# Reading a resident filter in place: a strided moving operand instead of packed copies in an FFT convolution beside a feed-forward block

## The chip, the cores and the metric

The kernel runs on one core of one Trainium2 chip. The metric is the device time of one execution in microseconds; the time of a kernel is the median over several runs.

## The reference

Two branches start from the same input and are added to it. Branch A gates a shifted input with `v`, convolves it along the sequence with a filter as long as the sequence, and gates the result with the normalised input. Branch B is a feed-forward block with ReLU. S = 2048 positions, D = 576 channels, Dff = 4608, all in float32.

```python
x = A_q
xn = layernorm(x)                       # no scale, no shift
# branch A
k_shift = sum(shift(k, t) * shift_k[:, 3 - t])  # causal, 4 taps
kv = k_shift * v
y = irfft(rfft(kv, 2*S) * rfft(ssm_k, 2*S))[:S] + kv * ssm_D
a = xn * y
# branch B
b = relu(xn @ w1) @ w2                  # 576 -> 4608 -> 576
out = x + a + b
```

## The kernel before, in words

Branch B fills TensorE (PE) from the start to the end. It runs in 36 "quads" `g` (18 slices of Dff, for each half of the positions). Each quad computes hidden values into the PSUM tiles `psh` (from the operands `x`, `xs`, `hl` and the split weights `wa` to `wd`, `wr`), splits them with ACT into `hh` and with DVE into `ll`, and multiplies them with the split second weight `w` into `pso`; DVE or ACT adds that to `acc`. Weights come on POOL's DMA queue (`load_w1`, `load_w2`) and are split by ACT (L512) and POOL (L513). DVE adds the weight sums (L525) and, at L684, `u`, which ACT at L686 and L591 needs before PE can go on with the next `psh`. L669 copies `psh` into `p`. L722 and L742 move `acc` into PSUM and back for some units.

Branch A is a generator, `conv()` with `stages()`. It runs between the matmuls of branch B: `tick` counts the columns that PE is given (`clock["ffn"]`) and takes the next step of the generator when its share is due. A step that yields a positive number costs so much of the share; a negative number is a pause of so many columns (`PAUSE` is 16,000); the word "wide" asks for a place where a PSUM slot can be borrowed. `here()` ties a step's instructions behind the latest ones of branch B on DVE and ACT.

All working memory of branch A is one SBUF tile, `area`, cut by offset into views that change from stage to stage. The stages that matter here:

- **Filter transform.** The filter lies resident in `kt`, as 288 channels by `A2` = 32 time residues, the residue innermost: element `t2` of all channels is a column with a step of 32 floats, 128 bytes. The two halves of the partitions hold the two halves of the channels. The loop over the 32 elements copies one after the other (odd ones on DVE at L918, even ones on ACT at L920) into one of four packed buffers `copies[e]`. Eleven filter groups follow behind the copies, each of up to 864 columns of the 32 x 288: `group` transforms them with float32 matmuls of 64x64 (L762) and the matrices `mats` into two PSUM tiles `psf` and the borrowed pair `psg`. ACT (L844) and DVE (L846) copy the results into the one buffer `z`, and SP's queue stores `z` to `zk` in HBM (L887). A piece of a group that ends at an element's border is split: 288 and 144 columns make up a full half of 432.
- **Input transform.** `load(t)` brings rows of `k` and `v` on ACT's queue for t up to 1 and on SP's after that, and for t up to 0 a row of `shift_k` on POOL's. These rows lie over `kt`. `tap` (L938, L941, L942) and `gate` (L946) make the gated input on DVE, and `input_group` transforms it through the same `group`, with stores to `zx` (L954).
- The products, the way back and the output follow; the change does not touch them.

`load(0)` stands behind the last copy of the filter, ahead of the last two filter groups in the code; the other loads come after the last group.

Of the kernel before, what the change touches and what calls it, by code (L numbers as in the profile page):

```python
# [12 lines left out]
AF = mybir.ActivationFunctionType  # L13
# [8 lines left out]
KS = 4  # L22
T = S // P
NH = D // 2
# [14 lines left out]
A2 = U * T  # L39
# [15 lines left out]
CW = 512  # L55
NCH = NG * D // CW
KG = 432
# [8 lines left out]
KT = 0  # L66
ROWS = 2 * KS + 8
REST = ROWS * D
Z, KSO, WT = REST, REST + 4 * CW, REST + 4 * CW + 4 * NH
AREA = WT + 4 * U * P  # L70

OPERANDS = ("00", "01", "s2", "s3", "11", "s1", "s4")
# [27 lines left out]
def h3_ffn_kernel(ctx: ExitStack, tc, x, k, v, shift_k, ssm_k, ssm_D, w1, w2, fwd, inv, mid, out):  # L100
    nc = tc.nc
    x = x[0].rearrange("(p u t) d -> u p t d", u=U, t=T)
    k = k[0].rearrange("(p u t) d -> u p t d", u=U, t=T)
# [28 lines left out]
    def at_t(z, t):  # L132

        return z[:, t].rearrange("q g d -> g q d")
# [5 lines left out]
    def fft_psum():  # L140
        return ps_f.tile([P, 512], F32, tag="f", name="psf")
# [4 lines left out]
    def borrowed():  # L146

        return ps_o.tile([P, 2, 512], F32, tag=f"o{slot['closed']}", name="psg")
# [12 lines left out]
    def move(tile_, rows, t, store=False, queues=(nc.sync, nc.sync)):  # L161
        for u in range(U):
            a, b = tile_[halves(u)[0]], rows[u, :, t]
            queues[u].dma_start(*((b, a) if store else (a, b)))
# [87 lines left out]
    @contextmanager  # L252
    def here():


        with tc.issue_after(done["acc"].ins), tc.issue_after(done["act"].ins):
            yield
# [502 lines left out]
    def in_turn(ps, a, m, start, stop):  # L760
        with tc.issue_after(done["pe"].ins):
            done["pe"] = nc.tensor.matmul(ps, a, m, start=start, stop=stop, skip_group_check=True)  # L762
# [35 lines left out]
    def stages(view, views):  # L798


        kt = view(KT, NH, A2)
# [6 lines left out]
                with here():  # L808
                    nc.scalar.dma_start(kt[halves(h)[0], d:d + KD, :], src)  # L809

        z = view(Z, 2, 2 * CW)
        mats = Ring(*views(WT, 4, U, P))

        def load_mat(key, t):
            nc.gpsimd.dma_start(mats.put(key), fwd[t])

        def group(parts, most, engines):


            wide = borrowed()  # L820
            sets = [[fft_psum() for _ in range(2)], [wide[:, r, :] for r in range(2)]]
            ends = []
            for pieces, banks in zip(parts, sets):
                off = 0
                for w, mat, src in pieces:
                    for k in range(2):
                        for r in range(2):
                            in_turn(banks[r][sides[r ^ k], off:off + w],
                                    mat(r)[sides[r], A1 * (r ^ k):A1 * (r ^ k) + A1],
                                    src[sides[r]], off == 0, True)  # L830
                    off += w
                ends.append(off)
            if ends[-1] < NH or len(ends) == 1:
                unwritten.add(slot["closed"])
            for n, off in enumerate(ends):
                to = z[:, :, n * most:n * most + off]
                if n and engines == ("act", "act"):
                    with here():
                        nc.scalar.activation(to, wide[:, :, :off], AF.Copy)
                    continue  # L840
                for r in range(2):
                    with here():
                        if engines[r] == "act":
                            nc.scalar.activation(to[:, r, :], sets[n][r][:, :off], AF.Copy)  # L844
                        else:
                            nc.vector.tensor_copy(to[:, r, :], sets[n][r][:, :off])  # L846

        def divided(a, b, most, step):

            parts = []  # L850
            while a < b:
                end, off = min(a + most, b), 0
                parts.append([])
                while a < end:
                    e, c = divmod(a, step)
                    w = min(end - a, step - c)
                    parts[-1].append((e, c, w, off))
                    a, off = a + w, off + w
            return parts
# [4 lines left out]
            yield -KT_GAP  # L864
        for t in range(2):
            load_mat(("k", t), t)
        copies = Ring(*views(KSO, 4, NH))
        skip = copies.put("skip")
        for h in range(2):
            nc.sync.dma_start(skip[h * A1:h * A1 + 1, :], ssm_D[None, h * NH:(h + 1) * NH])  # L870
        yield -PAUSE
# [4 lines left out]
        order = [T * u + t for t in range(T) for u in range(U)]  # L876
        flat = A2 * NH
        starts = list(range(0, flat, 2 * KG))

        def filter_group(a):  # L880
            parts = divided(a, min(a + 2 * KG, flat), KG, NH)
            group([[(w, lambda r, u=order[e] // T, t=order[e] % T: mats["k", t][:, u, :],
                     copies[e][:, c:c + w]) for e, c, w, _ in part] for part in parts],
                  KG, ("act", "dve"))
            for e, c, w, off in divided(a, min(a + 2 * KG, flat), flat, NH)[0]:
                for r in range(2):
                    nc.sync.dma_start(at_t(zk, order[e])[:, :, r * NH + c:r * NH + c + w],  # L887
                                      z[:, r, off:off + w])
# [4 lines left out]
        sums = Ring(*rows[11:15])  # L893
        terms = Ring(*rows[15:16])

        def load(t):

            w = win[t] if t < 2 else win.put(t)
            if t <= 0:
                nc.gpsimd.dma_start(sk[:, -t, :], shift_k[-t:1 - t, :].to_broadcast([P, D]))  # L900
            if t >= 0:
                queues = (nc.sync if t > 1 else nc.scalar,) * 2
                with here():
                    move(w, k, t, queues=queues)
                    move(gates.put(t), v, t, queues=queues)
            else:
                with here():
                    nc.vector.memset(w[0:1, :], 0.0)
                    nc.scalar.dma_start(w[1:A1, :], k[1, 0:A1 - 1, T + t, :])
                    nc.scalar.dma_start(w[A1:, :], k[0, :, T + t, :])  # L910
# [1 line left out]
        for t in range(1 - KS, 2):  # L912
            win.put(t)
        for e, t2 in enumerate(order):
            to = copies.put(e)
            with here():
                if e % 2:
                    nc.vector.tensor_copy(to, kt[:, :, t2])  # L918
                else:
                    nc.scalar.activation(to, kt[:, :, t2], AF.Copy)  # L920
            if e == A2 - 1:
                load(0)
            yield W_FK / 2
            while starts and min(starts[0] + 2 * KG, flat) <= e * NH + (e == A2 - 1) * NH:
                yield "wide"
                filter_group(starts.pop(0))
                yield W_FK / 2 / (len(range(0, flat, 2 * KG)) / A2)
            if e % U and e // U + 2 < T:
                load_mat(("k", e // U + 2), e // U + 2)
# [14 lines left out]
        def gate(t):  # L944
            with here():
                nc.vector.tensor_tensor(sums[t], sums[t], gates[t], OP.mult)  # L946

        def input_group(j):
            parts = divided(2 * j * CW, 2 * (j + 1) * CW, CW, D)
            group([[(w, lambda r, t=t: mats["x", t][:, r, :], sums[t][:, c:c + w])  # L950
                    for t, c, w, _ in part] for part in parts], CW, ("act", "act"))
            for t, c, w, off in divided(2 * j * CW, 2 * (j + 1) * CW, T * D, D)[0]:
                for r in range(2):
                    nc.sync.dma_start(at_t(zx, T * r + t)[:, :, c:c + w], z[:, r, off:off + w])  # L954

        for t in (*range(-1, -KS, -1), 1):
            load(t)
            yield -PAUSE / 4
        for t in range(2):
# [3 lines left out]
        for t in range(T):  # L963
            for n in range(KS + 1):
                if n < KS:
                    tap(t, n)
                    yield W_FX * (2 if n else 1)
                else:
                    gate(t)
                    if t + 2 < T:  # L970
                        load(t + 2)
                    yield W_FX
                if n == 1 or t == T - 1 and n == KS:
                    last = t if n == KS else t - 1
                    while made_groups < n_groups and (2 * CW * (made_groups + 1) - 1) // D <= last:
                        yield "wide"
                        input_group(made_groups)
                        made_groups += 1
                        yield 2 * W_FX
                    if n == 1 and 2 <= t + 1 < T:  # L980
                        load_mat(("x", t + 1), t + 1)
# [108 lines left out]
        order = [*range(HT, T), *range(HT)]  # L1090
# [213 lines left out]
```

## Time and profile before

| | |
|---|---|
| median of 3 runs | 1029.08 us (1028.98 to 1030.45) |
| profiled execution, own time | 1038.15 us |
| its span, first to last instruction | 1036.3 us |
| mean granted TensorE clock | 0.996 |
| PE busy | 1019.9 us, 98% of the span |
| DVE, ACT, POOL busy | 702.4, 431.4, 463.6 us |
| L920, 16 copies on ACT | 11.7 us, mean 731 ns |
| L918, 16 copies on DVE | 9.3 us, mean 591 ns |

A row of a group reads: line, engine, operation, output tile, input tiles, shape, count, then busy time in us and the mean of one in ns, then the idle time of the engine ahead of it and what ended it. Rows of a timeline begin with the start and the duration in us. PEld is the loading of weights, which overlaps PE. A row of the chain has start, duration and what ran. Matmuls of 64x64 on different corners of the array run side by side, so their durations overlap.

### The profile page before, as it was taken

To read this page: it belongs to the slowest core of one execution; us is meant where nothing else is said; L and a number is where in the kernel's file an instruction comes from. 1 tells how busy PE (TensorE), PEld (TensorE's weight loads), DVE (VectorE), ACT (ScalarE), POOL (GpSimd) and SP (SyncE) were. 2 spreads that over 40 slices of the span, in tenths; PEclk is the share of its full clock that TensorE was granted. 3 is DMA by queue.
4 is the path that set the end of the run, shared out by engine and by line. 5 is a ranking of instruction groups with operands and counts; after the bars stand their busy time and mean duration, and the time that the engine had idled before them with its cause. 6 is when DMAs were issued, how large, how long until landed. Compare 5 with 4: busy or idle time off the path is not lost.

```text
span 1036.3 us, 17434 instructions
## 1 busy us (share of the span) xinstructions
PE 1019.9 (98%) x6506; PEld 846.6 (82%) x6506; DVE 702.4 (68%) x1075; ACT 431.4 (42%) x770; POOL 463.6 (45%) x502
## 2 busy tenths in 40 slices
PE   8999999999999999989999999999999999999997
PEld 5898999998988888878878888866777777788777
DVE  6787677775565556778787889455666666556764
ACT  7244334443354444434444444544444445332120
POOL 3335444555443555544555455314424245244450
PEclk9999999999999999998999999999999999999999
DMA  7114364479445473379944433677877887757684
GB/s 175 52 49 118 114 162 126 154 216 199 115 127 172 160 245 104 126 216 322 277 139 132 129 103 115 210 221 227 242 212 226 250 256 226 221 177 230 208 259 114
DMA packets 130848, 184.69 MB, mean 178 GB/s; under 512 B 69213, under 2 KB 81631, under 8 KB 129868
## 3 DMA queue, kind: packets, MB, share of 16 engines
q1 hardware_dynamic: 76180, 123.48, 39.9%
q0 software_dynamic: 16048, 52.44, 16.9%
q10 hardware_dynamic: 38536, 7.66, 3.9%
q8 instruction: 51, 0.84, 0.3%
q14 instruction: 33, 0.27, 0.1%
HBM read 119.04 MB, written 45.61 MB: 159 GB/s over the span
## 4 chain that ended last, share of the span: by engine, by line
PE 88%; DMA 4%; DVE 3%; ACT 2%; issue 1%; POOL 1%; ACTq 1%; SPq 0%; DVEq 0%; POOLq 0%
PE pso L569 40%; PE psh L569 34%; PE psf L762 6%; PE psg L762 4%; PE psh_c L569 3%; DMA r<-in_w 2%; DMA zk<-area 1%; DMA acc<-in_x 1%; ACTq L809 0%; DVE area L1047 0%; DVE area L941 0%; DVE area L942 0%; ACT x L291 0%; DMA area<-in_k 0%; DVE sums L525 0%
## 5 line engine op out<-in xcount | busy, mean ns | idle before, releaser
L569 PE MATMUL pso<-w,hh 128*128 128x288 f32 x2304 | 467.9, 296 | 0.0
L569 PEld LDWEIGHTS pso<-w,hh 128*128 128x128 f32 x2304 | 378.1, 188 | 35.9 <-issue 14.8
L569 PE MATMUL pso<-w,ll 128*128 128x288 f32 x1152 | 339.5, 295 | 0.0
L749 DVE TENSOR_TENSOR acc<-pso,acc 128x576 f32<-128x576 f32 x243 | 183.1, 754 | 167.3 <-PE pso L569 166.9
L569 PEld LDWEIGHTS pso<-w,ll 128*128 128x128 f32 x1152 | 216.4, 188 | 0.0
L513 POOL TENSOR_TENSOR wb<-sums,wb 128x512 fp32r<-128x512 f32 x33 | 52.4, 1587 | 251.1 <-ACT wb L512 217.9
L513 POOL TENSOR_TENSOR w<-r,w 128x576 fp32r<-128x576 f32 x72 | 108.2, 1510 | 118.6 <-ACT w L512 118.6
L569 PE MATMUL psh<-xs,wb 128*128 128x512 f32 x396 | 102.7, 394 | 0.0
L569 PE MATMUL psh<-x,wa 128*128 128x512 f32 x396 | 102.5, 394 | 0.1
L569 PE MATMUL psh<-hl,wr 128*128 128x512 f32 x264 | 85.7, 406 | 3.6 <-ACT psh L686 3.1
L569 PEld LDWEIGHTS psh<-x,wa 128*128 128x128 f32 x396 | 72.4, 188 | 15.3 <-ACT psh L648 0.5
L569 PEld LDWEIGHTS psh<-xs,wb 128*128 128x128 f32 x396 | 70.6, 188 | 14.6 <-issue 3.2
L513 POOL TENSOR_TENSOR wa<-r,wa 128x512 fp32r<-128x512 f32 x36 | 56.1, 1558 | 57.2 <-ACT wa L512 57.1
L762 PE MATMUL psf<-area 64*64 64x512 f32 (+10 forms) x664 | 75.2, 489 | 1.6 <-DVE area L1047 1.0
L593 DVE SCALAR_TENSOR_TENSOR ll<-psh,hh 128x512 fp32r<-128x512 f32 x66 | 45.2, 685 | 37.6 <-ACT hh L591 37.2
L686 ACT ACTIVATE psh<-psh 128x512 f32<-128x512 f32 x33 | 19.2, 582 | 116.5 <-DVE u L684 114.6
L569 PEld LDWEIGHTS psh<-hl,wr 128*128 128x128 f32 x264 | 46.3, 189 | 23.0 <-issue 10.5
L591 ACT ACTIVATE hh<-psh 128x512 fp32r<-128x512 f32 x66 | 39.3, 596 | 50.8 <-PE psh L569 50.1
L1020 ACT ACTIVATE area<-psg 128x1024 f32<-128x1024 f32 x34 | 33.0, 1024 | 53.7 <-PE psg L762 53.7
L591 ACT ACTIVATE hh<-p 128x512 fp32r<-128x512 f32 x33 | 20.9, 632 | 81.9 <-PE pso L569 46.9
L569 PE MATMUL psh<-xs,wd 128*128 128x512 f32 x198 | 52.6, 401 | 0.0
L1047 DVE TENSOR_TENSOR area<-psf,area 128x512 f32<-128x512 f32 x72 | 44.7, 682 | 11.6 <-DMA area<-area 8.4
(134 smaller groups left out, 1487.0 us busy)
## 6 DMA issues: line engine op xcount, KB each, us to landing
r<-in_w POOLq DMA_DIRECT2D x70, 288.0 KB, 3.8
area<-area SPq DMA_DIRECT2D x144, 128.0 KB, 4.0
r<-in_w POOLq DMA_DIRECT2D x35, 512.0 KB, 4.8
zk<-area SPq DMA_DIRECT2D x64, 144.0 KB, 2.2
area<-zk SPq DMA_DIRECT2D x18, 512.0 KB, 4.5
area<-zx SPq DMA_DIRECT2D x18, 512.0 KB, 4.1
zy<-area SPq DMA_DIRECT2D x36, 256.0 KB, 4.7
area<-zy SPq DMA_DIRECT2D x32, 288.0 KB, 4.3
```

The source lines that it names most:

```text
L513: nc.gpsimd.tensor_tensor(w[:, 1, :n], src, w[:, 0, :n], OP.subtract)
L569: last = nc.tensor.matmul(ps, a, m, start=start and n == 0, stop=n == len(seq) - 1, skip_group_check=True)
L591: done["act"] = nc.scalar.activation(hh, ps, AF.Relu)
L593: nc.vector.scalar_tensor_tensor(ll, ps, 0.0, hh, op0=OP.max, op1=OP.subtract)
L686: nc.scalar.activation(x, y, AF.Copy, scale=-1.0)
L749: done["acc"] = nc.vector.tensor_tensor(two(acc[t]), ps[:, :, :NH], two(acc[t]), OP.add)
L762: done["pe"] = nc.tensor.matmul(ps, a, m, start=start, stop=stop, skip_group_check=True)
L1020: nc.scalar.activation(dst, src, AF.Copy)
L1047: nc.vector.tensor_tensor(filt[:, c, k, :], banks[k], filt[:, c, k, :], OP.mult)
```

## The change

The copies go. The matmuls of a filter group take `kt[:, c:c + w, order[e]]` as their moving operand. The space of `copies` and the old `z` becomes two result buffers of 2 x 864 floats for the filter groups, `zs`; the input groups keep one of 2 x 1024 (`one`). `skip`, the row of `ssm_D`, moves to the start of that space. A filter group is now due with its last element, not one element later. `load(0)` moves behind the last filter group, to the other loads, each of which is followed by a pause of `PAUSE / 4`.

```diff
-Z, KSO, WT = REST, REST + 4 * CW, REST + 4 * CW + 4 * NH
+Z, WT = REST, REST + 8 * KG
...
-        z = view(Z, 2, 2 * CW)
+        zs = Ring(*views(Z, 2, 2, 2 * KG))
...
-        def group(parts, most, engines):
+        def group(zs, parts, most, engines):
...
+            z = zs.put("z")
...
+            return z
...
-        copies = Ring(*views(KSO, 4, NH))
-        skip = copies.put("skip")
+        skip = view(Z, NH)
...
-            group([[(w, lambda r, u=order[e] // T, t=order[e] % T: mats["k", t][:, u, :],
-                     copies[e][:, c:c + w]) for e, c, w, _ in part] for part in parts],
+            z = group(zs, [[(w, lambda r, u=order[e] // T, t=order[e] % T: mats["k", t][:, u, :],
+                     kt[:, c:c + w, order[e]]) for e, c, w, _ in part] for part in parts],
                   KG, ("act", "dve"))
...
         for e, t2 in enumerate(order):
-            to = copies.put(e)
-            with here():
-                if e % 2:
-                    nc.vector.tensor_copy(to, kt[:, :, t2])
-                else:
-                    nc.scalar.activation(to, kt[:, :, t2], AF.Copy)
-            if e == A2 - 1:
-                load(0)
             yield W_FK / 2
-            while starts and min(starts[0] + 2 * KG, flat) <= e * NH + (e == A2 - 1) * NH:
+            while starts and min(starts[0] + 2 * KG, flat) <= (e + 1) * NH:
...
+        one = Ring(view(Z, 2, 2 * CW))
...
-            group([[(w, lambda r, t=t: mats["x", t][:, r, :], sums[t][:, c:c + w])
+            z = group(one, [[(w, lambda r, t=t: mats["x", t][:, r, :], sums[t][:, c:c + w])
...
-        for t in (*range(-1, -KS, -1), 1):
+        for t in (*range(0, -KS, -1), 1):
             load(t)
             yield -PAUSE / 4
```

What the change moves in the engines' order is shown at three places; the last number of a name is that of its buffer. The first is ACT's order around the end of the filter transform, before and then after; L844 and L845 are the copies of the last two groups' results, L920 the last copy of the filter, L164 the loads of `load(0)`.

```order
L920 ACTIVATE area<-area 128x288
L844 ACTIVATE area<-psf 128x432
L844 ACTIVATE area<-psg 128x432
L591 ACTIVATE hh_1_0_3929<-psh_4_3792 128x512
L512 ACTIVATE wc_3963<-sums_3773 128x512
L648 ACTIVATE psh_2_3934<-psh_1_3933 128x512
L164 DMA area<-in_k 64x576 x2
L164 DMA area<-in_v 64x576 x2
L844 ACTIVATE area<-psf 128x432
L844 ACTIVATE area<-psg 128x144
L591 ACTIVATE hh_0_0_4011<-psh_1_3933 128x512
```

After the change, the same stretch of ACT's order:

```order
L845 ACTIVATE area<-psf 128x432
L845 ACTIVATE area<-psg 128x432
L591 ACTIVATE hh_1_0_3898<-psh_4_3793 128x512
L512 ACTIVATE wc_3926<-sums_3774 128x512
L648 ACTIVATE psh_2_3903<-psh_1_3902 128x512
L845 ACTIVATE area<-psf 128x432
L845 ACTIVATE area<-psg 128x144
L591 ACTIVATE hh_0_0_3974<-psh_1_3902 128x512
L164 DMA area<-in_k 64x576 x2
L164 DMA area<-in_v 64x576 x2
L512 ACTIVATE w_3997<-r_14_0_3658 128x576
```

The copy is gone, and the two rows of loads stand behind the last group's results and behind `hh_0_0`, ahead of the next weight split.

The second is DVE's order in quad 19, from the first weight sum of quad 20 to `u` of quad 19. The rows on `area` are taps and the gate of the input transform (L941, L942, L946 before; L934, L935 after).

```order
L525 TENSOR_TENSOR sums20_5447<-r1_20_5268 128x256 x2
L942 TENSOR_TENSOR area_1173<-area_1173 128x576
L525 TENSOR_TENSOR sums20_5447<-sums20_5447,r1_20_5268 128x256
L941 TENSOR_TENSOR area_1173<-area_1173 128x576
L525 TENSOR_TENSOR sums20_5447<-sums20_5447,r1_20_5268 128x256
L942 TENSOR_TENSOR area_1173<-area_1173 128x576
L941 TENSOR_TENSOR area_1173<-area_1173 128x576
L942 TENSOR_TENSOR area_1173<-area_1173 128x576
L946 TENSOR_TENSOR area_1173<-area_1173 128x576
L684 TENSOR_TENSOR u2_19_5393<-psh19_5_5413,u2_19_5393 128x512
```

After the change, the same stretch of DVE's order:

```order
L525 TENSOR_TENSOR sums20_5413<-r1_20_5208 128x256 x2
L935 TENSOR_TENSOR area_1173<-area_1173 128x576
L525 TENSOR_TENSOR sums20_5413<-sums20_5413,r1_20_5208 128x256
L934 TENSOR_TENSOR area_1173<-area_1173 128x576
L525 TENSOR_TENSOR sums20_5413<-sums20_5413,r1_20_5208 128x256
L935 TENSOR_TENSOR area_1173<-area_1173 128x576
L684 TENSOR_TENSOR u2_19_5358<-psh19_5_5376,u2_19_5358 128x512
```

Six operations on `area` stood there, and three stand there now; the same count goes from one to six in quad 20.

The third is PE's order in quad 17, where the second input group stood between two products of the feed-forward block.

```order
L569 MATMUL psh17_2_4724<-xs3_746,wb17_4682 128x512 x6
L762 MATMUL psf_4870<-area_1173 64x128
L762 MATMUL psf_4871<-area_1173 64x128
L762 MATMUL psf_4870<-area_1173 64x128
L762 MATMUL psf_4871<-area_1173 64x128
L762 MATMUL psf_4870<-area_1173 64x384
L762 MATMUL psf_4871<-area_1173 64x384
L762 MATMUL psf_4870<-area_1173 64x384
L762 MATMUL psf_4871<-area_1173 64x384
L762 MATMUL psg_4869<-area_1173 64x192 x4
L762 MATMUL psg_4869<-area_1173 64x320 x4
L569 MATMUL psh17_5_4835<-hl0_861,wr17_4688 128x512 x2
```

After the change, PE's order from the unit ahead of it on:

```order
L569 MATMUL pso16_4_4780<-w216_4493,hh16_1_0_4682 128x288 x2
L569 MATMUL pso16_4_4780<-w216_4493,ll16_1_0_4683 128x288
L569 MATMUL pso16_4_4780<-w216_4585,hh16_1_1_4638 128x288 x2
L569 MATMUL pso16_4_4780<-w216_4585,ll16_1_1_4639 128x288
L569 MATMUL psh17_2_4687<-xs3_746,wb17_4642 128x512 x6
L569 MATMUL psh17_5_4800<-hl0_861,wr17_4648 128x512 x2
L569 MATMUL psh17_5_4800<-xs4_916,wd17_4645 128x512 x6
```

The product of `xs3` is now followed directly by `psh17_5<-hl0`; the second input group comes 12,032 columns of branch B later, behind `psh17_2<-hl1`. The first one comes 6,528 columns later than before, and the filter groups keep their places or come up to 12,032 columns earlier.

## The prediction

> **What bounds the kernel now.** I read the busy shares first, then the chain that ended last, then the table of stages.
>
> ```profile
> PE 1019.9 (98%) x6506; PEld 846.6 (82%) x6506; DVE 702.4 (68%) x1075; ACT 431.4 (42%) x770; POOL 463.6 (45%) x502
> ...
> PE 88%; DMA 4%; DVE 3%; ACT 2%; issue 1%; POOL 1%; ACTq 1%; SPq 0%; DVEq 0%; POOLq 0%
> ```
>
> ```profile
> 280.00:380.00 100.00, 100.00 (x831) 83.25 (x830) 59.27 (x99) 46.13 (x87) 49.10 (x61) 1.00 0.51 161
> ...
> 434.00:665.00 231.00, 225.58 (x1470) 195.43 (x1469) 179.97 (x239) 103.02 (x183) 116.37 (x112) 0.99 0.58 180
> ```
>
> The stage rows give the stretch, then busy time of PE, PEld, DVE, ACT and POOL, the granted clock, the DMA share and GB/s. The first stretch holds the whole filter transform: PE is busy for 100.00 of 100.00 us. There, time moves only if PE's own work gets longer or shorter. The second holds the input transform, and PE lacks 5.4 us in it. Its two large waits are these:
>
> ```profile
> PE psg L762 <- ACT acc L742: 2.9, 1, 2.9
> PE psh L569 <- ACT psh L686: 2.6, 1, 2.6
> ```
>
> **Price of one column of the transform.** This is the timeline of PE in the first filter group.
>
> ```profile
> 287.64 0.96 PE L762 MATMUL psf<-area 64*64 64x288 f32 x16
> 288.42 0.91 PE L762 MATMUL psg<-area 64*64 64x144 f32 x16
> 289.26 0.40 PE L569 MATMUL pso<-w,hh 128*128 128x288 f32 x1
> ```
>
> Each logical fp32 matmul leaves two records, and the four 64x64 matmuls of a piece run side by side. So the 432 columns into psf are 864 steps of four matmuls, and the psg matmuls start 0.78 us after them: 0.903 ns a step. All 32 elements of 288 columns are 9,216 columns, 18,432 steps, 16.6 us. The window's row for these matmuls agrees (PE, then PEld busy):
>
> ```profile
> 280.00:380.00 100.00, 18.15 (x344) 10.75 (x344) 1.00 0.51 161
> ```
>
> **Part 1: the moving operand with a step of 128 bytes.** Before, `copies[e]` is contiguous; after, the same steps read `kt[:, c:c+w, order[e]]`, one float of every 32. No matmul of the trace reads like that. The copies themselves do, on two other engines, and contiguous rows of the same engines stand beside them.
>
> ```profile
> L920 ACT ACTIVATE area<-area x16: 692/730/762, 285.1 to 367.3; 128x288 f32<-128x288 f32 x16
> ```
>
> ```profile
> L918 DVE COPY area<-area x16: 430/464/1683, 285.1 to 373.1; 128x288 f32<-128x288 f32 x16
> ```
>
> ```profile
> L512 ACT ACTIVATE wc<-sums 128x512 fp32r<-128x512 f32 x33 | 20.7, 626 | 0.1
> ...
> L512 ACT ACTIVATE wr<-r 128x256 fp32r<-128x256 f32 x36 | 14.5, 404 | 0.0
> ...
> L846 DVE COPY area<-psg 128x432 f32<-128x432 f32 x10 | 6.1, 607 | 4.8 <-ACT area L844 4.7
> ...
> L846 DVE COPY area<-psg 128x144 f32<-128x144 f32 x1 | 0.3, 298 | 0.0
> ```
>
> ACT, contiguous: (626 - 404)/256 = 0.867 ns an element, so 288 elements should take 432 ns. The strided copy takes 730 (least 692): 1.04 ns an element more (least 0.90), a pace of 1.77 to 1.90 ns, 2.0 to 2.2 times the contiguous one. DVE, from PSUM: (607 - 298)/288 = 1.07 ns an element and 144 ns fixed; the strided copy's 464 ns is then 1.11 ns an element, so at DVE's pace nothing shows.
>
> PE's step of 0.903 ns is nearest to ACT's 0.867, so I go by ACT. Its least row, a doubling, gives +0.903 ns x 18,432 = **+16.6 us**; its median gives 1.04 x 18,432 = +19.2. If PE only came down to DVE's strided pace, it would be (1.11 - 0.903) x 18,432 = +3.8. Zero is possible too: an fp32 step may leave the read port idle for half its time. The trace does show denser reads on PE: the matmuls of the feed-forward part (`pso`), with 288 contiguous columns each.
>
> ```profile
> 285.77 0.43 PE L569 MATMUL pso<-w,hh 128*128 128x288 f32 x2
> 286.03 0.29 PE L569 MATMUL pso<-w,ll 128*128 128x288 f32 x1
> ```
>
> Two of them in 0.26 us are 0.45 ns a column, half the fp32 step. A gain is excluded: the same number of steps is issued. I take 16.6 and keep 0 and 19.2 for the range. All of it lies on PE, where the stage has no idle time to absorb it.
>
> The Trainium skill ("Advanced Engine Details and Errata", Memory Cachelines) says that SBUF has lines of 16 bytes, that two hits on a line are needed to hide the access, and that a new line at every access costs; it gives no price. ACT's rows agree and DVE's neither show nor exclude it. By this rule the sum is the +16.6 above. In the other direction, "FP8 and Floating Point Precision" (TensorE Precision Notes) of the Trainium skill says that true FP32 takes four passes through the array; the two records a matmul and the step of twice 0.45 ns agree. If one read serves two passes, the sum would be 0.
>
> **Part 2: what is removed.** 16 ACT copies (16 x 731 ns = 11.7 us) and 16 DVE copies (9.3 us busy). They ran beside a PE that was never idle. ACT's copies held PEld for 0.4 us in all:
>
> ```profile
> DVE area L846 <- DMA zk<-area: 8.6, 4, 3.6
> ...
> PEld psh L569 <- ACT area L920: 0.4, 1, 0.4
> ```
>
> I count 0, and -0.4 at best. The first row is what the second result buffer takes away: DVE waited 8.6 us for stores of the filter. Behind DVE waits PE's PSUM, but PE lost nothing there. What is late next on that path is the store itself, once:
>
> ```profile
> 377.49 10.36 DMA zk<-area
> ...
> 391.01 0.57 ACT psh L686
> 391.63 0.74 PE psh L569 x2
> ```
>
> PE lost 0.6 us at 391.6, through ACT, whose queue held a load. I count 0, at best -0.6.
>
> **Part 3: what moves.** `load(0)` issues two loads of k and two of v on ACT's queue and one `shift_k` load on POOL's. It now stands behind the last group and `hh_0_0`, and a pause of `PAUSE / 4` = 4,000 column counts follows it.
>
> ```profile
> 373.58 1.19 ACTq L164 DMA_DIRECT2D area<-in_k  x2
> 374.81 1.29 ACTq L164 DMA_DIRECT2D area<-in_v  x2
> 376.32 0.53 ACT L844 ACTIVATE area<-psf 128x432 f32<-128x432 f32 x1 [4.52 <-PE psf L762]
> ```
>
> The 2.5 us of issue stood in a gap of 4.5 us in which ACT waited for PE. Now they stand ahead of the split `w` and the copy `u`, at worst 2.5 us late, once. On POOL's queue the `shift_k` loads keep their place; they now wait for PE's last group instead of the last copy; by the fence above, that group is over at 376.3. I count 0, at worst +1. The first input group moves 6,528 columns down PE's order and the next ones 1,000 to 14,000, at 0.45 ns up to 6 us, so the two waits of that stage meet other neighbours.
>
> The first wait is in quad 17. The load of `w1` took 11.48 us while the DMA engines were 94% busy, ACT stood behind it, and PE's granted clock averaged 0.87 over the 20 us:
>
> ```profile
> 452.37 11.48 DMA r<-in_w
> ...
> 464.47 0.58 ACT p L669
> 465.05 0.55 ACT acc L742
> 465.64 1.99 PE psg L762 x16
> ```
>
> ```profile
> 450.00:470.00 20.00, 17.14 (x108) 13.47 (x107) 12.87 (x17) 8.44 (x14) 11.42 (x12) 0.87 0.94 312
> ```
>
> The input group that stood there has moved behind `hl1`, but the next matmul, `psh17_5<-hl0`, needs `p` of L669, which ends 0.6 us ahead of L742 in the same queue. The wait stays within 1 us. The second is in quad 19, where DVE came late to `u`:
>
> ```profile
> 524.54 0.77 DVE area L941
> ...
> 525.33 0.77 DVE area L942
> ...
> 526.80 0.69 DVE u L684
> ...
> 527.52 0.59 ACT psh L686
> ...
> 528.15 0.74 PE psh L569 x2
> ```
>
> The order has six conv operations between the first `sums` and `u` there before, and three after: 3 x 0.77 = -2.3 us. In quad 20 it has one before and six after, which may bring the same wait back: +2.6 at most. I count 0 for both, -2.3 to +2.6.
>
> **Sum.** +16.6 and zeros. The profiled execution took 1038.15 us, 0.9% over the 1029.08 us median, so it would read 1054.8; part of its two waits may be its own. On the median: 1029.08 + 16.6 = **1045.7 us**.
>
> **Rivals.**
> 1. The read hides under the fp32 step, and the moves even out: 1029, within 0.2% (2 us, about what can be told from no change). For it: PE's denser contiguous reads. Against it: ACT, at nearly the same pace, pays.
> 2. Faster, on the other side: the read hides, the wait of quad 19 loses its 2.3 us and the late store its 0.6: 1026.2. It decides while the read costs under 2.9 us / 18,432 = 0.16 ns a step.
> 3. A small price, DVE's pace: 1029.08 + 3.8 = 1032.9, with other paces up to 1040.
> 4. The two matmuls that share 64 partitions take turns at ACT's strided pace: 2 x 1.90 - 0.903 = 2.9 ns a step more, +53 us, 1082. Contiguous reads show no taking of turns.
> 5. The read hides, but quad 20 waits: 1029.08 + 2.6 = 1031.7.
>
> **Chances.** Halved pace (1040 to 1051) 0.46; rival 1 0.14; rival 2 0.15; rival 3 0.12; rival 5 0.07; rival 4 or anything over 1051 0.06. Faster is rival 2: 0.15. Same is rival 1: 0.14. Slower is the rest: 0.71. The range runs from 1027, inside rival 2, to 1029.08 + 19.2 + 2.6 = 1051, and leaves out most of rival 2's tail and rival 4. The likeliest case alone would be 1040 to 1051.
>
> **What would show it.** The psf part of a full filter group should take 1.56 us instead of 0.78, and the stage's L762 matmuls about 35 us instead of 18. L918 and L920 are gone, and DVE's wait for zk with them. If psf to psg stays at 0.78 us, part 1 is wrong, and the waits of quads 17, 19 and 20 decide the rest.

## The result, and the profile after

The changed kernel takes 1052.77 us (median of 4 runs, 1052.22 to 1053.83). The kernel before took 1029.76 us beside it (median of 4 runs, 1028.98 to 1032.16). The ratio is 1.0224, with a 95% interval of 1.0211 to 1.0237: 23.0 us slower, where 16.6 were predicted. The forecast time of 1045.7 us is 7.1 us short, and the result lies 1.8 us over the range.

The profiled execution of after took 1053.83 us, with a span of 1052.0 us. The two spans, 1052.0 and 1036.3 us, differ by only 15.7 us, because the profiled execution of before was 9 us slower than its runs. The 23.0 us of the timed runs are the measure. This is the profile page of after: the busy row of PE, and the chain that ended last.

```profile
PE 1040.1 (99%) x6506; PEld 853.0 (81%) x6506; DVE 698.9 (66%) x1059; ACT 421.7 (40%) x754; POOL 459.0 (44%) x502
...
PE 32%; DVE 0%; ACT 0%; issue 0%; DVEq 0%
```

PE runs the same 6,506 matmuls and is busy for 20.2 us more (1040.1 - 1019.9). The chain could be followed back over only a third of the span here, so it says little beyond "PE". The windows carry more: first the two stretches that the prediction looked at, then the rows of L762 alone.

```profile
280.00:380.00 100.00, 100.00 (x688) 74.57 (x687) 42.57 (x69) 32.62 (x61) 39.95 (x49) 1.00 0.40 127
434.00:665.00 231.00, 230.07 (x1494) 201.31 (x1493) 194.23 (x254) 104.97 (x189) 122.72 (x121) 1.00 0.57 176
```

```profile
280.00:405.00 125.00, 38.02 (x344) 17.37 (x344) 1.00 0.42 129
```

In the first 100 us PE is busy all the time, as before, but gets 688 matmuls done instead of 831. The second stretch lost its two large waits: PE lacks 0.9 us in it, not 5.4. The 344 matmuls of the filter transform are busy for 38.02 us instead of 18.15, and their weight loads for 17.37 instead of 10.75. That is 19.9 us more on the engine that bounds the kernel. The first group of the filter, in the timeline of PE:

```profile
291.58 1.90 PE L762 MATMUL psf<-area 64*64 64x288 f32 x16
293.08 1.92 PE L762 MATMUL psg<-area 64*64 64x144 f32 x16
294.93 0.54 PE L569 MATMUL pso<-w,hh 128*128 128x288 f32 x2
```

The psf part takes 1.50 us (293.08 - 291.58) where it took 0.78, and the psg part 1.85 (294.93 - 293.08) where it took 0.84 (289.26 - 288.42). Together 3.35 us stand against 1.62 for the same 1,728 steps.

PE's largest waits after the change:

```profile
PE psh L569 <- ACT u L663: 2.0, 1, 2.0
...
PE psh L569 <- ACT psh L686: 0.9, 2, 0.5
```

The first is new. It stands in quad 9, while the filter is still being loaded. ACT's timeline there, after the change:

```profile
239.94 2.56 ACTq L809 DMA_DIRECT2D area<-in_ssm_k  x1
242.54 0.69 ACT L512 ACTIVATE w<-r 128x576 fp32r<-128x576 f32 x1 [1.99 <-issue]
242.57 2.56 ACTq L809 DMA_DIRECT2D area<-in_ssm_k  x1
245.17 0.60 ACT L663 ACTIVATE u<-psh 128x512 f32<-128x512 f32 x1 [1.94 <-issue]
```

And before the change:

```profile
241.54 2.56 ACTq L809 DMA_DIRECT2D area<-in_ssm_k  x1
242.08 0.58 ACT L663 ACTIVATE u<-psh 128x512 f32<-128x512 f32 x1
```

The issue of this filter load keeps ACT's queue for 2.56 us. Before, `u` was queued ahead of the last of three such loads; its work started 0.54 us into that load's issue. After, `u` stands behind the load and starts when the issue is over, and PE waits 2.0 us for it. `skip` stands at another place in `area` now, and its load on SP's queue starts at 203 us instead of 235; the second experiment below shows that this place decides the order of `u` and the load.

The matmuls behind that wait ran slowly in this execution. The packed kernel of the first experiment has nearly the same wait, and there the same six matmuls took 1.67 us. First after, then the packed kernel:

```profile
245.82 2.82 PE L569 MATMUL psh<-xs,wb 128*128 128x512 f32 x6 [2.01 <-ACT u L663]
```

```profile
245.23 1.67 PE L569 MATMUL psh<-xs,wb 128*128 128x512 f32 x6 [1.92 <-ACT u L663]
```

### The profile page after: what moved, and what is told of

It is laid out like the page before. It is cut to its first block, busy times and chain, and to the rows that moved or that the text cites. A ratio compares the mean times of both kernels' runs of the same rounds, so it can differ in the third digit from the quotient of the medians.

```text
span 1052.0 us, 17406 instructions
## 1 busy us (share of the span) xinstructions
PE 1040.1 (99%) x6506; PEld 853.0 (81%) x6506; DVE 698.9 (66%) x1059; ACT 421.7 (40%) x754; POOL 459.0 (44%) x502
## 5 line engine op out<-in xcount | busy, mean ns | idle before, releaser
L762 PE MATMUL psf<-area 64*64 64x512 f32 (+10 forms) x664 | 85.1, 550 | 0.1
L513 POOL TENSOR_TENSOR wa<-r,wa 128x512 fp32r<-128x512 f32 x36 | 52.6, 1462 | 50.1 <-ACT wa L512 50.0
L686 ACT ACTIVATE psh<-psh 128x512 f32<-128x512 f32 x33 | 19.2, 582 | 111.2 <-DVE u L684 110.3
L762 PE MATMUL psg<-area 64*64 64x512 f32 (+10 forms) x496 | 56.8, 516 | 0.3 <-DVE acc L749 0.2
L1015 ACT ACTIVATE area<-psg 128x1024 f32<-128x1024 f32 x34 | 33.0, 1024 | 54.4 <-PE psg L762 47.0
L591 ACT ACTIVATE hh<-p 128x512 fp32r<-128x512 f32 x33 | 20.9, 632 | 83.3 <-DVE p L691 43.6
```

The costliest lines, as they stand in the source:

```text
L513: nc.gpsimd.tensor_tensor(w[:, 1, :n], src, w[:, 0, :n], OP.subtract)
L591: done["act"] = nc.scalar.activation(hh, ps, AF.Relu)
L686: nc.scalar.activation(x, y, AF.Copy, scale=-1.0)
L1015: nc.scalar.activation(dst, src, AF.Copy)
```

## Experiments

The time of after has two candidates: the strided read itself, and the order on ACT's queue around the loads. Each experiment changes one of them. Where several were timed together, they share their runs of before.

### The read's step alone

```diff
+        packed = view(KT, A2, NH)
...
-                     kt[:, c:c + w, order[e]]) for e, c, w, _ in part] for part in parts],
+                     packed[:, order[e], c:c + w]) for e, c, w, _ in part] for part in parts],
```

> The changed kernel with one edit: the filter matmuls read 288 floats that lie one behind the other in kt instead of every 32nd (other elements than the filter's, so the result is not the convolution). PE, DVE, ACT and SP keep exactly the order of the changed kernel. Theory (the read's step is the price, plus a separate 3 us from ACT's order in quad 9): the 344 recorded L762 matmuls of the filter stage fall back from 37 to 17 us and the time falls by 19.9 us, to about 1033, and stays 3 us over the kernel before. Rival (the read explains all 23 us): about 1030. Rival (moved groups and loads cost most): above 1040.

Measured: 1031.89 us (median of 10 runs) against 1029.09 for before (13 runs); ratio 1.0029 [1.0015, 1.0043]. The theory was met (1033 expected). The transform's matmuls and PE's wait in this kernel:

```profile
280.00:405.00 125.00, 18.11 (x344) 10.80 (x344) 1.00 0.53 165
```

```profile
PE psh L569 <- ACT u L663: 1.9, 1, 1.9
```

With a step of one float the 344 matmuls are back at 18.11 us. After took 20.9 us more than this kernel (1052.77 - 1031.89, from two sets of runs); with each kernel measured against its own set's runs of before, the difference is 20.2 us (23.0 - 2.8). The step of the read costs that. What is left, 2.8 us over before, is not the read. The wait of quad 9 is still there, so it belongs to the order and not to the read.

### Is the wait in quad 9 the rest?

```diff
-        skip = view(Z, NH)
+        skip = view(Z + 4 * CW, NH)
```

This puts `skip` back to its old place, and with it `u` of quad 9 ahead of the filter load.

> The changed kernel with one edit: skip lies where it lay before (2048 floats behind Z). In the built order this puts u of quad 9 (L663) back ahead of the fourth filter load on ACT's queue; PE and DVE keep the changed kernel's order. Theory: PE's wait for u in quad 9 (2.0 us and the half clock behind it) goes, 3 us less: about 1049.6. Rival (that wait is an accident of one profile): 1052.8, no difference.

Measured: 1053.52 us (4 runs), ratio to before 1.0239 [1.0223, 1.0254]; no difference from after that the runs could tell. The expectation missed. The wait for `u` in quad 9 is gone (one of 0.6 us for `p` is left there), but a larger one has come up in quad 14, where the first loads of the input stand. The waits of PE, and ACT's timeline there:

```profile
PE psh L569 <- ACT p L669: 2.5, 2, 1.9
```

```profile
401.49 0.57 ACTq L910 DMA_DIRECT2D area<-in_k  x1
401.50 0.65 ACT L722 ACTIVATE pso<-acc 128x576 f32<-128x576 f32 x1
407.18 0.48 ACTq L911 DMA_DIRECT2D area<-in_k  x1
407.76 0.60 ACT L669 ACTIVATE p<-psh 128x512 f32<-128x512 f32 x1 [5.62 <-DMA zk<-area]
```

The load of `k` at L911 waits on ACT's queue for a store of the filter (`zk<-area`) to land. `p`, which stands behind it, starts 5.62 us late. In the chain, the store's end and the load's issue follow each other:

```profile
397.72 9.44 DMA zk<-area
...
407.18 0.48 ACTq L911
```

The load does not touch what that store reads: its rows lie over `kt`, and `z` lies behind them. What they share is a semaphore. The loads and stores of SP's and ACT's queues take eight semaphores (DMAHW0 to 7) by turns, and each waits for the earlier transfer on its own. These are the two instructions in the kernel's instruction lists, SP's store first:

```
137 L888 DMA zk_90<-area_1173 32x4x288 [waits DMAHW5_49,DVE_49]
...
307 L911 DMA area_1173<-in_k 64x576 [waits DMAHW5_49]
308 L669 ACTIVATE p5_14_4036<-psh14_5_4025 128x512 [waits PE_49,Activation_49]
```

PE, which needs `p`, stands still for 1.88 us and then runs slowly:

```profile
404.99 1.55 PE L569 MATMUL psh<-xs,wb 128*128 128x512 f32 x6
408.41 0.84 PE L569 MATMUL psh<-hl,wr 128*128 128x512 f32 x2 [1.88 <-ACT p L669]
409.05 2.77 PE L569 MATMUL psh<-xs,wd 128*128 128x512 f32 x6
```

```profile
408.00:412.00 4.00, 3.59 (x10) 2.90 (x11) 0.08 (x1) 2.10 (x4) 2.62 (x2) 0.61 0.58 174
```

The six matmuls behind the wait take 2.77 us; the six ahead of it took 1.55. The window's row has a granted clock of 0.61 for these 4 us. So this stall of 1.9 us was followed by a loss of 1.2 us more (2.77 - 1.55), as the one in quad 9 of after was (2.82 us). Not every stall is: behind 1.92 us in the packed kernel the six took 1.67 us. What decides it is not shown. In the profile of after, the same loads stand there too, but ACT was idle for only 2.74 us, and PE did not wait. ACT's row there:

```profile
408.31 0.60 ACT L669 ACTIVATE p<-psh 128x512 f32<-128x512 f32 x1 [2.74 <-DMA zk<-area]
```

So this kernel's profile has a wait in quad 14 in place of the one in quad 9, and its runs show no gain.

### Moving load(0) alone

Before, with copies and one `z`, and only `load(0)` moved behind the last group.

```diff
-            if e == A2 - 1:
-                load(0)
...
-        for t in (*range(-1, -KS, -1), 1):
+        for t in (*range(0, -KS, -1), 1):
```

> The kernel before with the third part of the change alone: load(0) behind the last filter group, copies and the one result buffer kept. Theory: no difference (within 2 us of the kernel before), because ACT's queue has room there. Rival (the later input stage meets worse neighbours and costs the 3 us left over): 1032 to 1034.

Measured: 1034.08 us (4 runs), ratio 1.0051 [1.0034, 1.0068]: 5.0 us slower than before, with contiguous reads. The theory of no difference missed; the time lies just above the rival's 1032 to 1034. PE's waits:

```profile
PE psh L569 <- ACT psh L686: 2.4, 2, 1.6
PE psh L569 <- ACT p L669: 1.4, 1, 1.4
```

The second row is the wait of quad 14 again. ACT's `p` came 5.00 us late behind the same load, held by the same store: they share DMAHW5 in this kernel too. ACT's timeline:

```profile
386.77 0.48 ACTq L910 DMA_DIRECT2D area<-in_k  x1
387.29 0.60 ACT L669 ACTIVATE p<-psh 128x512 f32<-128x512 f32 x1 [5.00 <-DMA zk<-area]
```

The move is not free. It puts the input's loads behind the last stores of the filter in the turns of the semaphores, and directly ahead of `p`. The rest of the 5.0 us stays open: the first row is two waits of 1.56 and 0.81 us some 300 us later, at 685.74 and 722.10 us, in a stretch where the profile of before has two other waits, of 0.85 and 0.57 us.

### The queue of the input's loads

Two kernels: after with `skip` in its old place and the first input loads on SP's queue instead of ACT's; and the same with the packed read of the first experiment.

```diff
-                queues = (nc.sync if t > 1 else nc.scalar,) * 2
+                queues = (nc.sync,) * 2
...
-                    nc.scalar.dma_start(w[1:A1, :], k[1, 0:A1 - 1, T + t, :])
-                    nc.scalar.dma_start(w[A1:, :], k[0, :, T + t, :])
+                    nc.sync.dma_start(w[1:A1, :], k[1, 0:A1 - 1, T + t, :])
+                    nc.sync.dma_start(w[A1:, :], k[0, :, T + t, :])
```

> The changed kernel with skip at its old place (as in x2_skip_place) and with the first input loads (t up to 1) on SP's queue instead of ACT's. Theory (the 3 us that the read does not explain are waits of ACT's queue on loads: quad 9 behind a filter load, quad 14 behind a k load that waits for a store of zk): both are gone, 1052.8 - 3 to 4 = about 1049, 19.9 over the kernel before. Rival (those waits are hidden or replaced): no difference from 1052.8 to 1053.5.

> x5_loads_on_sp with the packed read of x1_packed_inplace (288 floats one behind the other, other elements than the filter's, so the result is not the convolution). Theory: without the read's price and without the two waits of ACT's queue the changed kernel is no slower than the kernel before: 1028 to 1029.5. Rival (moved groups cost 3 us): 1031.9 as in x1_packed_inplace.

Measured: 1051.21 us (4 runs, ratio 1.0214 [1.0196, 1.0233]) with the strided read, and 1029.82 us (12 runs, ratio 1.0005 [0.9995, 1.0016]) with the packed one, against 1029.56 for before (23 runs). The strided kernel comes out between its theory (1049) and the rival; the packed one lies 0.3 us over its theory's 1028 to 1029.5. In the strided kernel the input's loads no longer hold ACT: no wait is left in quad 14, and the 0.4 us for `p` stand in quad 9.

```profile
PE psh L569 <- ACT psh L686: 2.0, 2, 1.5
...
PE psh L569 <- ACT p L669: 0.4, 1, 0.4
```

The pair differs by 21.4 us: the read again, measured without the two queue waits. The packed kernel holds everything else of the change (no copies, two result buffers, late loads) and is as fast as before. So the removed copies show no gain. The queue waits are most of what was left: 2.1 us between the packed kernels (1031.89 - 1029.82), 1.6 us between after and the strided one (1052.77 - 1051.21). These differences are between sets of runs, and in each pair the 95% intervals overlap, so all that can be said is that the queue waits are worth 1 to 3 us. The two waits of the first row, at 703.63 and 738.83 us, are not among those removed.

### What one column costs, by its step

After, with another step between the floats for each of the eleven filter groups; everything else stays.

```diff
+        steps = (1, 2, 3, 4, 6, 8, 16, 32, (32, 1), 31, 24)
+
+        def column(a, e, c, w):
+            s = steps[a // (2 * KG)]
...
+                return view(KT, NH, n)[:, c:c + w, e % n] if n > 1 else view(KT + c, w)
```

> The changed kernel with a different step of the moving operand in each filter group: 1, 2, 3, 4, 6, 8, 16, 32 floats, then a group in which one of the two matmuls on the same partitions steps by 32 and the other by 1, then 31 and 24 floats (other elements than the filter's, so the result is not the convolution). Same order on every engine. Theory (a price for every read of a new 16-byte line): steps of 1 and 2 cost 0.84 to 0.9 ns a column, 4 and more all cost about 1.97, 31 and 24 no less than 32. Rival (power-of-two banks): 31 and 24 cheap, 32 dear, the price growing with the power of two. The mixed group: 1.9 if each matmul is paced by its own reads, 1.2 to 1.5 if the two on the same partitions take turns.

One execution: 1046.63 us. The first rows of five groups, in the timeline of PE, with steps of 1, 2, 3, 4 and 32 floats:

```profile
288.44 0.96 PE L762 MATMUL psf<-area 64*64 64x288 f32 x16
289.22 0.91 PE L762 MATMUL psg<-area 64*64 64x144 f32 x16
...
296.21 0.99 PE L762 MATMUL psf<-area 64*64 64x288 f32 x16
297.03 0.94 PE L762 MATMUL psg<-area 64*64 64x144 f32 x16
...
306.57 1.37 PE L762 MATMUL psf<-area 64*64 64x288 f32 x16
307.75 1.34 PE L762 MATMUL psg<-area 64*64 64x144 f32 x16
...
315.63 1.74 PE L762 MATMUL psf<-area 64*64 64x288 f32 x16
317.17 1.72 PE L762 MATMUL psg<-area 64*64 64x144 f32 x16
...
356.97 1.94 PE L762 MATMUL psf<-area 64*64 64x288 f32 x16
358.53 2.06 PE L762 MATMUL psg<-area 64*64 64x144 f32 x16
360.53 0.53 PE L569 MATMUL pso<-w,hh 128*128 128x288 f32 x2
```

The distance from a psf row to its psg row is the time of 864 steps of four matmuls: 0.78, 0.82, 1.18, 1.54 and 1.56 us, or 0.90, 0.95, 1.37, 1.78 and 1.81 ns a step. Steps of 2 floats are nearly free, 4 floats cost all of the doubling, and the groups with 4, 6, 8, 16, 31 and 32 floats lie between 1.71 and 1.82 ns. So the theory of a price for each new line holds in shape, and the rival of power-of-two banks is out: 31 floats cost as much as 32. With 16-byte lines of four floats, the shares of reads that touch a new line at steps 1, 2, 3 and 4 are 1/4, 1/2, 3/4 and 1. A price of 1.79 ns a new line, fitted to the fourth group, or 0.90 ns a step where that is more, gives 0.90, 0.90, 1.34 and 1.79 ns. The Trainium skill ("Advanced Engine Details and Errata", Memory Cachelines) has the lines of 16 bytes and asks for two hits on each; the free step of 2 agrees. Another page of the Trainium skill ("SBUF — State Buffer", the note on SBUF cachelines) allows a stride of 4 fp32 for free; the 1.54 us of the fourth group differ, and the measurement decides.

The group with steps of 32 is also the one whose psg part is longest: 2.00 us (360.53 - 358.53), 2.31 ns a step, against 1.81 in its psf part. In the other groups with one step throughout the two parts differ less. In the mixed group, where one of the two matmuls on the same partitions stepped by 32 and the other by 1, the extra is missing:

```profile
366.67 1.43 PE L762 MATMUL psf<-area 64*64 64x288 f32 x14
...
369.74 0.73 PE L569 MATMUL psh<-hl,wr 128*128 128x512 f32 x2
```

This whole group took 3.07 us (369.74 - 366.67), 1.78 ns a step, against 3.56 us with 32 throughout (360.53 - 356.97) and 1.62 with 1. Taking turns was expected at 1.2 to 1.5 ns. So one dear operand brings the doubling, and at 32 what is above it came only where both operands stepped; why is open.

The last group, with a step of 24 floats, took 2.14 us for its psf part (2.48 ns a step), out of line with all others. Place or step? A second set put 24 first and, once more, last but one:

```diff
-        steps = (1, 2, 3, 4, 6, 8, 16, 32, (32, 1), 31, 24)
+        steps = (24, 32, (1, 4), (4, 1), 12, 20, 28, 30, 5, 24, 4)
```

> As x4_step_curve with the steps 24, 32, a group with 1 and 4 on the two matmuls of the same partitions, one with 4 and 1, then 12, 20, 28, 30, 5, 24 and 4 floats (other elements than the filter's, so the result is not the convolution). Theory (one price of about 1.8 ns for every new 16-byte line): 4, 5, 12, 20, 28, 30 at 1.8, 24 as well (its 2.5 ns in x4_step_curve came from the place), 32 at 1.8 to 2.0, the mixed groups at 1.8. Rival (the step itself matters beyond the line): 24 again at 2.5 in both places, and 12, 20, 28 between.

One execution: 1053.33 us. The first group, now with a step of 24:

```profile
288.61 2.35 PE L762 MATMUL psf<-area 64*64 64x288 f32 x16
290.75 2.38 PE L762 MATMUL psg<-area 64*64 64x144 f32 x16
```

It is the step, and the theory (the place) missed: 2.14 us here as there, and in the other place too. Steps of 5, 12, 28 and 30 floats gave 1.76 to 1.91 ns, and 20 gave 2.08. In the groups where one matmul of a pair read with a step of 4 and the other with 1, the whole group took 3.20 and 3.22 us, like a group with 4 throughout (3.19 us in the first set, 318.82 - 315.63): here, too, the dear operand sets the pace.

```diff
-        steps = (24, 32, (1, 4), (4, 1), 12, 20, 28, 30, 5, 24, 4)
+        steps = (22, 26, 18, 23, 25, 27, 20, 19, 21, 14, 10)
```

> The changed kernel with another step between the floats of the filter read for each of the eleven filter groups, in this order: 22, 26, 18, 23, 25, 27, 20, 19, 21, 14, 10 floats (other elements than the transform needs; every group's work and order stay). So far all steps from 4 floats on gave 1.71 to 1.91 ns a step of the matrix unit in the psf part, except 20 (2.08) and 24 (2.48, twice). Theory A: only the exact steps of 20 and 24 floats are dear, a matter of whole 16-byte lines that fall on each other; then 18, 19, 21, 22, 23, 25, 26, 27 give 1.8 to 1.9 ns, and 20 again 2.08. Rival B: the price rises over the whole neighbourhood of 24; then 22, 23, 25 and 26 lie between 2.1 and 2.5 ns and 18, 19, 21 between 1.85 and 2.2. Steps 10 and 14, which are not whole lines, give 1.7 to 1.9 by both. The time should be 1050 to 1058 us.

One execution: 1055.17 us. The groups with steps of 22, 23 and 25 floats:

```profile
291.23 2.18 PE L762 MATMUL psf<-area 64*64 64x288 f32 x16
293.20 2.19 PE L762 MATMUL psg<-area 64*64 64x144 f32 x16
...
323.56 2.27 PE L762 MATMUL psf<-area 64*64 64x288 f32 x16
325.62 2.29 PE L762 MATMUL psg<-area 64*64 64x144 f32 x16
...
334.46 1.75 PE L762 MATMUL psf<-area 64*64 64x288 f32 x16
336.02 1.75 PE L762 MATMUL psg<-area 64*64 64x144 f32 x16
```

In ns a step, psf part: 1.89 at 18 floats, 1.99 at 19, 2.08 at 20, 2.19 at 21, 2.28 at 22, 2.38 at 23, then 1.80 at 25, 1.92 at 26 and 1.99 at 27. With the 2.48 at 24 this is a ramp of 0.1 ns a float from 18 to 24 that falls back at 25. Theory A (only whole lines are dear) is out, and rival B is right up to 24 but not at 25 and 26. What makes the ramp stays open.

### Before, with its loads on SP's queue

The two queue waits point to a version of the kernel before: the filter's loads (L809) and the first input loads on SP's queue, nothing else.

```diff
-                    nc.scalar.dma_start(kt[halves(h)[0], d:d + KD, :], src)
+                    nc.sync.dma_start(kt[halves(h)[0], d:d + KD, :], src)
...
-                queues = (nc.sync if t > 1 else nc.scalar,) * 2
+                queues = (nc.sync,) * 2
```

> The kernel before with all loads of the filter and the first input loads on SP's queue. Theory: the 0.7 us of quad 9 and the 0.6 us of quad 14 that PE lost to ACT's queue in the profile before go: 1027.8, 0.1% faster. Rival: SP's queue, which then holds filter loads behind operand stores, delays something else: same or slower.

Measured: 1028.23 us (11 runs) against 1029.56 (23 runs), ratio 0.9986 [0.9975, 0.9996]. That is the forecast 0.1%: 1.3 us, and the interval only just leaves out no difference. The two waits that the profile of before has there, 0.36 us for `p` at 244.86 us and 0.56 us at 391.63 us, are gone.

Beside it, the packed kernel of the change takes 1.6 us more (1029.82 - 1028.23). It keeps the filter's loads on ACT's queue, and its profile has two waits for L686, 2.3 us together at 683 and 719 us, which this one does not have. The kernel with `load(0)` alone moved has such waits at 685.74 and 722.10 us, with the copies still in it. So "as fast as before" does not mean that the rest of the change is free: it may cost some 1.6 us, and which part of it does was not tested.

## Why the prediction was wrong, point by point

- **What bounds the kernel.** Right. PE was busy for 100.00 of 100.00 us in the stage before and after, so the longer matmuls went into the time in full: 19.9 us more in the rows, 20.2 to 21.4 us in the two timed pairs.
- **Part 1, mechanism.** Right. The psf part was forecast at 1.56 us; the full groups of after took 1.50 us (above) up to 1.63, and the step curve's group at 32 took 1.56. ACT's strided copy was the right neighbour; DVE's was not.
- **Part 1, size.** This is the first step that failed: +16.6 forecast, +19.9 in the rows. The term priced all 18,432 steps by the rise of the psf part, 0.903 ns. That was nearly right for psf and wrong for psg. Added up over the eleven groups, the psf parts (9,504 steps) rose by 8.9 us where this price gives 8.6, and the psg parts (8,928 steps) by 11.0 us where it gives 8.1. In the group shown, psg rose by 1.01 us (0.84 to 1.85). The prediction also took 16.6 us and the row's 18.15 us to agree; the 1.5 us between them are busy time of the same matmuls, and doubling the whole row would have given +18.15. Its 35 us for the stage's L762 matmuls came out at 38.02. ACT's median row (1.04 ns, +19.2) would have come within 0.7 us of the rows, but by luck: nothing in it is about the psg part. Why psg pays more than psf is open; the mixed group says only that the extra goes when one of the two operands is contiguous.
- **Part 2.** Nothing was forecast, and no gain shows: the packed kernel with the loads on SP's queue has no copies and two buffers, and takes the time of before (1.0005).
- **Part 3, and what stands ahead of it.** The second step that failed is a term that was never listed. The prediction put all that moves at 0, at worst +1, and followed the order at three places, all of them behind 280 us. In after, PE lost 2.01 us in quad 9, and 1.3 us more in the slow matmuls behind it (2.82 - 1.55). There `u` had slipped behind the issue of a filter load, 2.56 us long, about 130 us ahead of the first place that the prediction looked at. The cause is the move of `skip`, which the change makes and the prediction does not mention. At `load(0)` itself the forecast held in after, though not for its reason: ACT came 2.74 us late and PE did not wait. What holds ACT there is not the issue but the semaphore that a load shares with a filter store. With `skip` put back, the same place cost PE 1.88 us; with `load(0)` alone moved, ACT's `p` came 5.00 us late and the kernel took 5.0 us more. Together the queue waits are 1 to 3 us of the result.
- **The waits of quads 17 and 19.** Both are gone, and quad 20 did not get one. The forecast counted 0 and kept -2.3 to +2.6. On the median no gain shows, and the profile of the kernel before with its loads on SP's queue does not have these two waits either, though its diff does not touch quads 17 and 19; they may belong to the one profiled execution of before. The prediction's bare sum on that execution, 1054.8 us, lies nearer to the result than its forecast, by luck: that execution was 9 us slower than the timed runs.
- **Rivals.** Rivals 1, 2, 3 and 5 all need a cheap read, and the first experiment excludes that. Rival 4, matmuls that take turns on the same partitions, was priced at 1082 us and is out by the time itself and by the mixed groups, which go at the pace of their dear operand alone. No rival counted the loads on ACT's queue as a cost.

The sum of what was measured: 20 to 21 us for the read and 1 to 3 us for the queue waits make the 23.0 us. Nothing finer is settled, neither the split between the two nor that between the waits. Of the 7.1 us between forecast and result, 3.3 are the read's size, 0.7 are the runs of before (1029.76 instead of 1029.08), and the rest is the queue waits and what the rows of the read leave out.

## What to carry to other kernels

In this kernel a moving operand that takes one float of every 16 bytes or more doubled the time of its fp32 matmuls, so packing copies on engines with idle time were worth their instructions while TensorE was the bound; a step of two floats cost only 5% (0.95 instead of 0.90 ns). Price such a change over all its matmuls, not over the part that reads best. List everything that the change moves, a small load at the far end of the kernel too. A DMA on a compute engine's queue costs what it waits for, not only what it takes to issue: list for each moved load which transfers must land first, by data and by shared semaphore, and what stands behind it in that queue.

## What the runs showed of the hardware

- One fp32 column step of four 64x64 matmuls took 0.90, 0.95, 1.37 and 1.78 ns at steps of 1, 2, 3 and 4 floats in the psf part, and 1.71 to 1.92 ns at most steps above that.
- Steps of 18 to 24 floats rose from 1.89 to 2.48 ns and fell to 1.80 at 25; the cause is open.
- With 32 floats on one of the two matmuls of the same partitions and 1 on the other, a group took 3.07 us; with 32 on both, 3.56 us.
- After PE had stood still for 1.88 us, its next six matmuls took 2.77 instead of 1.55 us, at a granted clock of 0.61 over 4 us; after 2.01 us, 2.82 us. After 1.92 us in another run they took 1.67 us, so a stall of this length does not always bring the low clock.
- Nine of the sixteen filter loads of after, all of one shape, were issued in 0.60 to 0.67 us on ACT's queue. The seven that stood directly behind another one took 1.39 to 2.85 us.
